# Pooled attention and routed experts: pinned pooling of the last two batches, one routing step per chunk for the second pair, another buffer for the fourth row tile

## The chip, the core and the metric

The kernel runs on one core of a Trainium2 chip. A core has five engines that each work through a list of instructions in order and wait for each other by semaphores: TensorE (PE, matrix products; PEld is its weight load), VectorE (DVE), ScalarE (ACT), GpSimd (POOL) and SyncE (SP), which here only issues DMAs. DMAs issued by GpSimd take time on that engine; most of them here are indirect: a column of indices says which rows are read or written. The metric is device time in microseconds, the median of three runs.

## What is computed

Attention comes first, over 8 batches, 8 heads, 576 positions of 64 values, with keys and values averaged over 8 neighbours:

```python
k_p = k.reshape(B, H, Sp, pool, D).mean(axis=3)        # 576 -> 72 positions
v_p = v.reshape(B, H, Sp, pool, D).mean(axis=3)
scores = scale * np.matmul(q, k_p.transpose(0, 1, 3, 2))
attn = np.exp(scores - np.max(scores, axis=-1, keepdims=True))
attn = attn / (np.sum(attn, axis=-1, keepdims=True) + 1e-09)
attn_out = np.matmul(attn, v_p)
```

Its output, as 4608 tokens of 512 values, is routed to 2 of 8 experts. The two are the largest of `x @ w_gate + log1p(exp(x @ w_noise)) * noise`, their weights a softmax of the two values:

```python
for e in range(E):
    for k in range(2):
        mask = top2[:, k] == e
        h = np.maximum(x[mask] @ w1[e], 0.0)           # 512 -> 1024
        out[mask] += top2_w[mask, k, None] * (h @ w2[e])
```

## The kernel before

A scheduling layer takes the instructions in program order with priorities and writes one list for each engine; `tc.issue_after(x)` says that what is made inside it may not stand ahead of `x`. What decides at run time is the list of each engine and the semaphores.

**Attention.** The 8 batches go in 4 pairs (`pr` 0 to 3) of 9 chunks each, so chunk `i` runs from 0 to 35; chunks 9 to 17 are the second pair, 18 to 26 the third, 27 to 35 the last. A chunk is 128 query rows of one batch, or the 64 last rows of both batches of a pair. For each, TensorE makes scores (`qk`), VectorE their maxima (`mx`), ScalarE the exponentials, TensorE transposes and multiplies with the values (`et`, `av`), and VectorE normalises into `xr` (L419), which goes to `x_dram`, and into the routing logits `lg`.

Keys and values are pooled by VectorE adds: `k_prep` and `v_prep` call `pooled` (L241, L248), three steps for `k`, four for `v`. The batch's results are needed when its pair begins. A table `bg`, filled by `plan`, says in which chunk each step is handed to the scheduler, some chunks ahead of use. The loads of `k` and `v` have two buffers each. `k7` and `v7` are the last batch's.

**Routing.** `route` makes the top two experts of a pair's 1152 tokens: a list of some 50 small VectorE steps with four `yield`s, then a count of places by two matmuls `rk` (L575, L576) that need its step L554, then the positions `pos` (L600). It is advanced by `adv` once in every chunk of the following pair, by one or two steps. When it is through, 18 indirect DMAs from GpSimd (`scatter`, L603) write the token numbers and weights of the pair into `rec_dram`. They are queued in `scq` and handed out `ADV[pr]` per chunk. `load_recs` reads these records back: for the first expert's first tiles after the second pair, for its next tiles after the third, and for all experts after the last (its `late` part: `xf`, L653, on GpSimd; `px`, L647, on TensorE).

**Experts.** Each expert has 1216 token places: four row tiles (0 to 3), three (4 to 6), and tiles 7 to 9, of which the last is half. Expert 0 takes the groups in the order 0, 4, 7; the others 0, 7, 4. For a group, `fetch` gathers token rows `xg` from `x_dram` (L702: four quarter-row gathers a tile; GpSimd), `split` transposes them and makes high and low parts, `stage1` makes `ph` (L943; three buffers), from which ScalarE and VectorE make `hh` and `hl` (L949), and `stage2` makes `py`. Then the weighted sum is put into the output rows. For experts 1 to 7 the former rows are needed: `prev` gathers them (L963) into one of three buffers `pvb`, `finish` adds on VectorE (L980) and writes back by a scatter (L984). The group of tiles 7 to 9 has its own buffer `pv4` of ten quarter-row blocks: ten gathers (L998), ten sums (L1021), ten scatters (L1024). GpSimd issues all of these in the order of its list. A group of four tiles calls `prev` for the first three at its start, and for the fourth when the first has been written back.

Of the kernel before, what the change touches and what calls it, by code (L numbers as in the profile page):

```python
# [20 lines left out]
def kernel(  # L21
# [13 lines left out]
    B, H, S, D = q.shape  # L35
# [3 lines left out]
    P = 128  # L39
# [7 lines left out]
    NP = B // 2  # L47
# [83 lines left out]
    lastx, laste, lastt = [None], [None], [None]  # L131
# [4 lines left out]
    KO, VO, PO = (5,4,2)  # L136
# [19 lines left out]
    ADV = (3,3,3,4)  # L156
# [592 lines left out]
    def plan(i, f):  # L749
        bg.setdefault(max(0, i), []).append(f)  # L750

    def nxt(store, make, b):
        def f():
            if b not in store:
                store[b] = make(b)
            next(store[b], None)
        return f

    def k1_step():
        with tc.issue_after(v0_end[0].ins):  # L760
            nxt(kg, k_prep, 1)()
# [26 lines left out]
    for b in range(1, B):  # L788
        c = 9 * (b // 2) + (0 if b % 2 == 0 else 4)
        kd = c - 2  # L790
        for x in range(KSTEPS):
            plan(kd - KO + x, nxt(kg, k_prep, b) if b > 1 else k1_step)
        for x in range(VSTEPS):
            plan(kd - VO + x, nxt(vg, v_prep, b))
        for x in range(4):
            plan(kd - PO + x, nxt(pg, pe_prep, b))
    qtr(units[0], 0)
# [21 lines left out]
    for i, (ui, u, jj) in enumerate(chunks):  # L819
        pr, ci = divmod(i, NCH)  # L820
        if ci == 0:
            lgs[pr] = rp.tile([P, NCH, H, 2 * E], F32, tag="lg", name=f"lg{pr}")
        single = u[0] == "R"
        has = ui + 1 < NU
        if single:
            order = OR
        else:
            order = OD[jj]
        eT = None
        def bgs():  # L830
            for f in bg.get(i, ()):
                f()

        def adv():
            advance(2 if pr >= NP - 2 else 1, ADV[pr])

        for o in order + ("" if "b" in order else "b") + ("" if "x" in order else "x"):
            if o == "v" and i == 0:
                drain(pg[0])
            if o == "b":  # L840
                bgs()
            elif o == "x":
                adv()
            elif o == "e":
                eT, at = et(u, jj)
            elif o == "v":
                av(u, jj, ci, eT, at, lgs[pr])
            elif o in "012":
                if has:
                    qk(units[ui + 1], int(o))  # L850
            elif ui + 2 < NU:
                qtr(units[ui + 2], "qr".index(o))
        if i >= ZS and (i - ZS) % ZD == 0 and (i - ZS) // ZD < 36 // ZW:
            if ZA:
                with tc.issue_after(lastx[0].ins):
                    zero((i - ZS) // ZD)
            else:
                zero((i - ZS) // ZD)
        if pr == NP - 1 and ci == 0:
            for ih in ((0, 0), (0, 1), (1, 0)):  # L860
                wload(0, *ih)
            early_w = chain(weights(0, 0), weights(0, 1))
        if pr == NP - 1 and 3 <= ci < 6:
            with tc.issue_after(laste[0].ins), tc.issue_after(lastx[0].ins):
                next(early_w)
                next(early_w)
            if ci == 3:
                wload(0, 1, 1)
        if pr == 3 and ci == 4:
            fetch(groups[0])  # L870
        if ci == 4 and pr >= HS:
            gens.append(route(pr, 0, 5, lgs[pr], one))
        if ci == NCH - 1 and pr < NP - 1:
            gens.append(route(pr, 5 if pr >= HS else 0, NCH, lgs[pr], one))
# [48 lines left out]
    npv = [0]  # L923
# [33 lines left out]
        HT[grp] = hs  # L957

    def prev(e, t, np_):
        pv = pvb[npv[0] % 3]  # L960
        npv[0] += 1
        if e:
            g = nc.gpsimd.indirect_dma_start(  # L963
                out=pv[:np_], out_offset=None, in_=out,
                in_offset=bass.IndirectOffsetOnAxis(ap=tokc[e, t][:np_], axis=0),
                bounds_check=NTOK - 1, oob_is_err=False)
            tc.declare_no_dep(g.ins, group=f"out{e}", reason="rows of other tokens")
            tc.add_to_no_dep_group(f"out{e}", g.ins)
        return pv

# [2 lines left out]
    def finish(e, t, np_, y, pv):  # L973
# [4 lines left out]
        for u in range(4):  # L978
# [5 lines left out]
        s = nc.gpsimd.indirect_dma_start(  # L984
            out=out, out_offset=bass.IndirectOffsetOnAxis(ap=tokc[e, t][:np_], axis=0),
            in_=res[:np_], in_offset=None, bounds_check=NTOK - 1, oob_is_err=False)
        tc.declare_no_dep(s.ins, group=f"out{e}", reason="rows of other tokens")
        tc.add_to_no_dep_group(f"out{e}", s.ins)

    def stage2(grp, mid, hook=None):  # L990
        e, t0, nt = grp
# [2 lines left out]
        if t0 == 7:  # L994
# [22 lines left out]
            for i in range(10):  # L1017
# [4 lines left out]
                else:  # L1022
# [1 line left out]
                s = nc.gpsimd.indirect_dma_start(  # L1024
                    out=out4, out_offset=bass.IndirectOffsetOnAxis(ap=oi4[e, t0 + i // 4][:, i % 4], axis=0),
                    in_=r4[:, i], in_offset=None, bounds_check=4 * NTOK - 1, oob_is_err=False)
                tc.declare_no_dep(s.ins, group=f"out{e}", reason="rows of other tokens")
                tc.add_to_no_dep_group(f"out{e}", s.ins)
            return
        pvs = [prev(e, t, P) for t in range(t0, t0 + min(nt, 3))]  # L1030
        mid()
        for t in range(t0, t0 + nt):
            cs = slice((t - t0) * P, (t - t0 + 1) * P)
# [5 lines left out]
                                                start=(i == 0), stop=(i == 3 * NFB - 1))  # L1039
                    i += 1  # L1040
            finish(e, t, P, py, pvs.pop(0))
            if t + 3 < t0 + nt:
                pvs.append(prev(e, t + 3, P))
            if hook:
                hook(t - t0)

# [182 lines left out]
```

## Time and profile before

| | |
|---|---|
| median of three runs | 1074.07 us (1072.03 to 1075.58) |
| the profiled execution | 1070.93 us, its span 1068.8 us |
| mean granted clock of TensorE | 0.983 |
| busy: TensorE, VectorE, GpSimd | 95%, 53%, 59% of the span |

The span counts from the first to the last instruction of that one execution. A granted clock of 1.00 is 2.4 GHz, 0.50 is 1.2 GHz. A time in the rows counts from the start of the span. Matmuls are pipelined, so that the ends of neighbouring rows overlap by a little. The attention ends near 201 us; the experts take the rest.

### The profile page before, as it was taken

How to read it: one execution, taken by the hardware profiler on the slowest of the kernel's cores; microseconds unless marked ns; L12 is line 12 of the kernel's file. 1: busy time of each engine (PE TensorE's matmuls, PEld its weight loads, DVE VectorE, ACT ScalarE, POOL GpSimd, SP SyncE). 2: the span in 40 equal slices, each digit the busy share in tenths (PEclk: the TensorE clock that was granted, in tenths of full speed). 3: DMA queues.
4: the chain of work that ended last, by engine and by line, in shares of the span. 5: the costliest groups of instructions: out<-in, count | busy, mean ns of one | idle time of the engine just before them, and what ended most of it. 6: DMA issues, size and time to landing. Idle time of an engine off the chain costs nothing. (4 is left out here: it accounts for less than half of the span.)

```text
span 1068.8 us, 16011 instructions
## 1 busy us (share of the span) xinstructions
PE 1020.6 (95%) x5840; PEld 920.4 (86%) x5840; DVE 565.2 (53%) x1316; ACT 340.2 (32%) x857; POOL 634.7 (59%) x662
## 2 busy tenths in 40 slices
PE   6989599899999799999999999999999999999997
PEld 5888498679898699889988998898889889988995
DVE  6888867763365146435633554355525553554241
ACT  5777577611123023212330233122312231222110
POOL 4003653746767767775677577757775777677231
PEclk8999899999999989999999999999999999999999
DMA  9999997732434243523352335233433443232200
GB/s 275 301 306 270 250 293 243 145 99 53 125 80 137 68 124 80 170 65 121 85 169 69 116 91 160 84 102 112 143 92 93 110 135 121 66 106 82 69 19 31
DMA packets 76244, 140.63 MB, mean 132 GB/s; under 512 B 24453, under 2 KB 32730, under 8 KB 76164
## 3 DMA queue, kind: packets, MB, share of 16 engines
q1 hardware_dynamic: 47844, 76.82, 26.4%
q0 software_dynamic: 28320, 62.77, 20.2%
q8 instruction: 47, 0.77, 0.3%
q14 instruction: 33, 0.27, 0.1%
HBM read 102.27 MB, written 39.17 MB: 132 GB/s over the span
## 5 line engine op out<-in xcount | busy, mean ns | idle before, releaser
L943 PE MATMUL ph<-xh,w 128*128 128x384 f32 (+2 forms) x1536 | 408.0, 347 | 8.3 <-DVE hl L949 7.7
L702 POOL DMA_INDIRECT xg<-x_dram,x x266 | 259.4, 975 | 132.2 <-issue 67.3
L943 PEld LDWEIGHTS ph<-xh,w 128*128 128x128 f32 x1536 | 277.0, 189 | 29.2 <-DVE hl L949 7.9
L948 ACT ACTIVATE hh<-ph 128x512 fp32r<-128x512 f32 (+2 forms) x192 | 97.7, 509 | 576.0 <-PE ph L943 575.3
L1038 PE MATMUL py<-w,hh 128*128 128x512 f32 x896 | 276.6, 390 | 0.0
L943 PE MATMUL ph<-xl,w 128*128 128x320 f32 (+2 forms) x768 | 266.1, 346 | 0.0
L949 DVE SCALAR_TENSOR_TENSOR hl<-ph,hh 128x512 fp32r<-128x512 f32 (+2 forms) x192 | 111.1, 579 | 215.9 <-ACT hh L948 215.8
L1038 PEld LDWEIGHTS py<-w,hh 128*128 128x128 f32 x896 | 168.0, 188 | 34.4
L1038 PE MATMUL py<-w,hl 128*128 128x512 f32 x448 | 174.6, 390 | 0.0
L943 PEld LDWEIGHTS ph<-xl,w 128*128 128x128 f32 x768 | 145.6, 190 | 10.5 <-DVE xl L917 0.2
L980 DVE SCALAR_TENSOR_TENSOR pv<-py,raw,pv 128x128 f32<-128x128 f32 x196 | 54.9, 343 | 146.5 <-PE py L1038 104.5
L1024 POOL DMA_INDIRECT out_dram<-pv,o x80 | 85.5, 1069 | 49.7 <-DVE pv L1021 25.9
L1010 PE MATMUL py<-hh,w 128*128 128x320 f32 x512 | 112.8, 309 | 0.0
L603 POOL DMA_INDIRECT rec_dram<-rec,pos x72 | 75.8, 1053 | 48.0 <-DVE pos L600 21.6
L1038 PEld LDWEIGHTS py<-w,hl 128*128 128x128 f32 x448 | 84.1, 188 | 17.4
L477 DVE TENSOR_TENSOR w<-wst,w 128x512 fp32r<-128x512 f32 x128 | 87.9, 689 | 0.8 <-ACT w L476 0.3
L1010 PEld LDWEIGHTS py<-hh,w 128*128 128x128 f32 x512 | 85.6, 188 | 0.0
L998 POOL DMA_INDIRECT pv<-out_dram,o x70 | 71.4, 1019 | 21.3 <-issue 19.8
L984 POOL DMA_INDIRECT out_dram<-pv,raw x56 | 58.1, 1038 | 41.9 <-DVE pv L980 23.0
L476 ACT CAST w<-wst 128x512 fp32r<-128x512 f32 x128 | 77.3, 616 | 6.8 <-PE ph L943 2.9
L1010 PE MATMUL py<-hl,w 128*128 128x320 f32 x256 | 79.1, 309 | 0.0
L377 ACT ACTIVATE ex<-s,mx 128x72 f32<-128x72 f32 x288 | 69.8, 347 | 12.7 <-DVE mx L375 12.3
(154 smaller groups left out, 994.4 us busy)
## 6 DMA issues: line engine op xcount, KB each, us to landing
wst<-in_moe_w_dram SPq DMA_DIRECT2D x64, 512.0 KB, 3.8
v<-in_v_dram SPq DMA_DIRECT2D x24, 448.0 KB, 13.3
out_dram<-zt SPq DMA_DIRECT2D x9, 1024.0 KB, 21.8
k<-in_k_dram SPq DMA_DIRECT2D x7, 1280.0 KB, 16.5
q<-in_q_dram SPq DMA_DIRECT2D x7, 1024.0 KB, 19.3
x_dram<-xr POOLq DMA_DIRECT2D x12, 512.0 KB, 8.6
xg<-x_dram,x POOLq DMA_INDIRECT x276, 2.6
x_dram<-xr SPq DMA_DIRECT2D x4, 512.0 KB, 6.1
```

The source lines that it names most:

```text
L377: laste[0] = nc.scalar.activation(ex[:, jj, EPOS[h] * G:(EPOS[h] + 1) * G], sv[:, i], AF.Exp, bias=mx[:, i:i + 1])
L476: nc.scalar.copy(hv, sv)
L477: nc.vector.tensor_sub(lv, sv, hv.bitcast(F32))
L603: s = nc.gpsimd.indirect_dma_start(out=rec_dram[:, :], out_offset=bass.IndirectOffsetOnAxis(ap=pos[:, i, c:c + 1], axis=0), in_=rec[:, c, ...
L702: nc.gpsimd.indirect_dma_start(out=xg[:, r * P:(r + 1) * P], out_offset=None, in_=x4, in_offset=bass.IndirectOffsetOnAxis(ap=xi[e, t][:, r ...
L943: nc.tensor.matmul(ph[:, :n], w1s(e, a, db, f), xs[b][:, db, :n], start=(i == 0), stop=(i == 3 * NDB - 1))
L948: ra = nc.scalar.activation(hh[:, :n], ph[:, :n], AF.Relu)
L949: rd = hli[grp, f] = nc.vector.scalar_tensor_tensor(hl[:, :n], ph[:, :n], 0.0, hh[:, :n].bitcast(F32), op0=OP.max, op1=OP.subtract)
L998: g = nc.gpsimd.indirect_dma_start(out=pv4[:, i], out_offset=None, in_=out4, in_offset=bass.IndirectOffsetOnAxis(ap=oi4[e, t0 + i // 4][:, ...
L1010: nc.tensor.matmul(py[:, :n], w2s(e, b, f)[:, mb * P:(mb + 1) * P], hs[f][a][:, :n], start=(i == 0), stop=(i == 3 * NFB - 1))
L1024: s = nc.gpsimd.indirect_dma_start(out=out4, out_offset=bass.IndirectOffsetOnAxis(ap=oi4[e, t0 + i // 4][:, i % 4], axis=0), in_=r4[:, i], ...
L1038: lastm[0] = nc.tensor.matmul(py, hs[f][a][:, cs], w2s(e, b, f), start=(i == 0), stop=(i == 3 * NFB - 1))
```

## The change

There are three edits. In the first, the pooling steps of the last two batches (`b >= B - 2`) are made inside `issue_after(lx[max(lx) - 2])`: they may not stand ahead of the output `xr` of the chunk two before the one that hands them out. In the second, `adv` advances the routing by two steps per chunk in the last pair alone; in the pair before it, where the second pair is routed, by one. In the third, the former rows of the fourth row tile go into the first 512 columns of `pv4`, so that its `prev` can be issued with the other three; its scatter is put into a group of its own (`outb`), so that the ten quarter-row gathers, which overwrite `pv4`, wait for it.

```diff
--- before.py
+++ after.py
@@ -756,6 +756,14 @@
             next(store[b], None)
         return f
 
+    lx = {}
+
+    def pinned(f):
+        def g():
+            with tc.issue_after(lx[max(lx) - 2]):
+                f()
+        return g
+
     def k1_step():
         with tc.issue_after(v0_end[0].ins):
             nxt(kg, k_prep, 1)()
@@ -789,9 +797,9 @@
         c = 9 * (b // 2) + (0 if b % 2 == 0 else 4)
         kd = c - 2
         for x in range(KSTEPS):
-            plan(kd - KO + x, nxt(kg, k_prep, b) if b > 1 else k1_step)
+            plan(kd - KO + x, pinned(nxt(kg, k_prep, b)) if b >= B - 2 else nxt(kg, k_prep, b) if b > 1 else k1_step)
         for x in range(VSTEPS):
-            plan(kd - VO + x, nxt(vg, v_prep, b))
+            plan(kd - VO + x, pinned(nxt(vg, v_prep, b)) if b >= B - 2 else nxt(vg, v_prep, b))
         for x in range(4):
             plan(kd - PO + x, nxt(pg, pe_prep, b))
     qtr(units[0], 0)
@@ -832,7 +840,7 @@
                 f()
 
         def adv():
-            advance(2 if pr >= NP - 2 else 1, ADV[pr])
+            advance(2 if pr == NP - 1 else 1, ADV[pr])
 
         for o in order + ("" if "b" in order else "b") + ("" if "x" in order else "x"):
             if o == "v" and i == 0:
@@ -845,6 +853,7 @@
                 eT, at = et(u, jj)
             elif o == "v":
                 av(u, jj, ci, eT, at, lgs[pr])
+                lx[i] = lastx[0].ins
             elif o in "012":
                 if has:
                     qk(units[ui + 1], int(o))
@@ -957,14 +966,18 @@
         HT[grp] = hs
 
     def prev(e, t, np_):
-        pv = pvb[npv[0] % 3]
-        npv[0] += 1
+        if t == 3:
+            pv = pv4[:, :4].rearrange("p i c -> p (i c)")
+        else:
+            pv = pvb[npv[0] % 3]
+            npv[0] += 1
         if e:
             g = nc.gpsimd.indirect_dma_start(
                 out=pv[:np_], out_offset=None, in_=out,
                 in_offset=bass.IndirectOffsetOnAxis(ap=tokc[e, t][:np_], axis=0),
                 bounds_check=NTOK - 1, oob_is_err=False)
-            tc.declare_no_dep(g.ins, group=f"out{e}", reason="rows of other tokens")
+            for gr in (f"out{e}", f"outb{e}"):
+                tc.declare_no_dep(g.ins, group=gr, reason="rows of other tokens")
             tc.add_to_no_dep_group(f"out{e}", g.ins)
         return pv
 
@@ -984,8 +997,9 @@
         s = nc.gpsimd.indirect_dma_start(
             out=out, out_offset=bass.IndirectOffsetOnAxis(ap=tokc[e, t][:np_], axis=0),
             in_=res[:np_], in_offset=None, bounds_check=NTOK - 1, oob_is_err=False)
-        tc.declare_no_dep(s.ins, group=f"out{e}", reason="rows of other tokens")
-        tc.add_to_no_dep_group(f"out{e}", s.ins)
+        for gr in (f"out{e}", f"outb{e}"):
+            tc.declare_no_dep(s.ins, group=gr, reason="rows of other tokens")
+        tc.add_to_no_dep_group(f"outb{e}" if t == 3 else f"out{e}", s.ins)
 
     def stage2(grp, mid, hook=None):
         e, t0, nt = grp
@@ -1024,10 +1038,11 @@
                 s = nc.gpsimd.indirect_dma_start(
                     out=out4, out_offset=bass.IndirectOffsetOnAxis(ap=oi4[e, t0 + i // 4][:, i % 4], axis=0),
                     in_=r4[:, i], in_offset=None, bounds_check=4 * NTOK - 1, oob_is_err=False)
-                tc.declare_no_dep(s.ins, group=f"out{e}", reason="rows of other tokens")
+                for gr in (f"out{e}", f"outb{e}"):
+                    tc.declare_no_dep(s.ins, group=gr, reason="rows of other tokens")
                 tc.add_to_no_dep_group(f"out{e}", s.ins)
             return
-        pvs = [prev(e, t, P) for t in range(t0, t0 + min(nt, 3))]
+        pvs = [prev(e, t, P) for t in range(t0, t0 + nt)]
         mid()
         for t in range(t0, t0 + nt):
             cs = slice((t - t0) * P, (t - t0 + 1) * P)
@@ -1039,8 +1054,6 @@
                                                 start=(i == 0), stop=(i == 3 * NFB - 1))
                     i += 1
             finish(e, t, P, py, pvs.pop(0))
-            if t + 3 < t0 + nt:
-                pvs.append(prev(e, t + 3, P))
             if hook:
                 hook(t - t0)
```

What this does to the lists is shown at three places. The first is VectorE in the third pair, around L554 of the routing of the second pair (`rt1`). `k7` and `v7` are the last batch's loads, `rec1` the records' weights. Before:

```order
L241 TENSOR_TENSOR k7_1394<-k7_1394 128x5x256
L542 SCALAR_TENSOR_TENSOR rt1_0_15_1611<-eidx_111,rt1_0_15_1611 128x72
L565 TENSOR_SCALAR rt1_0_20_1688<-rt1_0_19_1622 128x9
L241 TENSOR_TENSOR k7_1394<-k7_1394 128x5x128
L543 TENSOR_REDUCE rt1_0_9_1598<-rt1_0_15_1611 128x9
L567 RECIPROCAL rec1_0_1619<-rt1_0_20_1688 128x9
L545 SCALAR_TENSOR_TENSOR rt1_0_16_1615<-eidx_111,rt1_0_9_1598 128x72
L568 TENSOR_TENSOR rec1_0_1619<-rec1_0_1619,rt1_0_19_1622 128x9
L241 TENSOR_TENSOR v7_1518<-v7_1518 112x3x256
L554 TENSOR_TENSOR rt1_0_17_1617<-rt1_0_12_1605,rt1_0_16_1615 128x72
L241 TENSOR_TENSOR v7_1518<-v7_1518 112x3x256
```

The same place after:

```order
L539 TENSOR_REDUCE rt1_0_14_1673<-rt1_0_13_1671 128x9
L241 TENSOR_TENSOR v6_1275<-v6_1275 112x6x128
L541 TENSOR_TENSOR rt1_0_15_1675<-rt1_0_13_1671,rt1_0_14_1673 128x72
L557 TENSOR_TENSOR rt1_0_18_1684<-rt1_0_14_1673,rt1_0_10_1663 128x9
L542 SCALAR_TENSOR_TENSOR rt1_0_15_1675<-eidx_111,rt1_0_15_1675 128x72
L414 TENSOR_SCALAR rd2_4_2_0_1803<-a2_4_2_0_1734 128x8
L543 TENSOR_REDUCE rt1_0_9_1662<-rt1_0_15_1675 128x9
L415 RECIPROCAL rd2_4_2_0_1803<-rd2_4_2_0_1803 128x8
L545 SCALAR_TENSOR_TENSOR rt1_0_16_1679<-eidx_111,rt1_0_9_1662 128x72
L419 TENSOR_TENSOR xr2_4_2_0_1806<-a2_4_2_0_1734,rd2_4_2_0_1803 128x512
L554 TENSOR_TENSOR rt1_0_17_1681<-rt1_0_12_1669,rt1_0_16_1679 128x72
L375 TENSOR_REDUCE mx2_5_0_2_1772<-s2_5_0_2_1769 128x4
```

The adds on `k7` and `v7` no longer stand ahead of L554; one on `v6` does. Chunk 22's output (`xr2_4_2_0`, L419), which before stood behind L554, now stands ahead of it.

The second place is TensorE, at the matmuls `rk1` that take L554's result. `a2_4_1_1` are the products of chunk 21, `a2_4_2_0` those of chunk 22. Before:

```order
L408 MATMUL a2_4_1_0_1625<-vbd0_168,eT2_4_1_0_1624 128x81 x2
L394 MATMUL a2_4_1_1_1722<-ident_69,ex2_4_1_0_1477 112x128 x2
L394 MATMUL a2_4_2_0_1770<-ident_69,ex2_4_2_0_1635 112x128 x2
L575 LDWEIGHTS ones_109
L575 MATMUL rk1_0_1694<-rt1_0_17_1617,ones_109 128x72
L576 LDWEIGHTS before_104
L576 MATMUL rk1_0_1694<-rt1_0_17_1617,before_104 128x72
L394 MATMUL ep2_4_1_1_0_1723<-ident_69,ex2_4_1_0_1477 112x128 x4
L344 MATMUL qp2_5_0_0_1734<-ident_69,q5_1272 128x128 x4
L408 MATMUL a2_4_1_1_1722<-vbd0_168,eT2_4_1_1_1721 128x162 x2
```

And after:

```order
L408 MATMUL a2_4_2_0_1734<-vbd0_168,eT2_4_2_0_1733 64x162 x4
L408 MATMUL a2_4_2_0_1734<-vbd0_168,eT2_4_2_0_1733 64x81 x2
L408 MATMUL a2_4_2_0_1734<-vbd1_170,eT2_4_2_0_1733 64x162 x4
L408 MATMUL a2_4_2_0_1734<-vbd1_170,eT2_4_2_0_1733 64x81 x2
L370 MATMUL s2_5_0_2_1769<-kbd1_166,qT2_5_0_1698 128x144 x2
L575 LDWEIGHTS ones_109
L575 MATMUL rk1_0_1818<-rt1_0_17_1681,ones_109 128x72
L576 LDWEIGHTS before_104
L576 MATMUL rk1_0_1818<-rt1_0_17_1681,before_104 128x72
L394 MATMUL ep2_5_0_0_0_1847<-ident_69,ex2_5_0_0_1744 112x128 x3
```

`rk1` has moved from ahead of chunk 21's products to behind those of chunk 22.

The third place is GpSimd in the first group of expert 2, as it stands in experts 2 to 6 alike: gathers of former rows into `pv0` to `pv2`, scatters to the output from them, the ten gathers into `pv4`, and row gathers `xg3` for expert 3. The first of the gathers of the group stands one row ahead. Before:

```order
L963 DMA pv0_2647<-out_0_dram,raw0_8_0_3095 128x512
L963 DMA pv1_2648<-out_0_dram,raw0_8_0_3095 128x512
L998 DMA pv4_2650<-out_0_dram,o0_8_0_3170 128x128 x10
L702 DMA xg3_0_5242<-x_dram_67,x0_8_0_3184 128x128 x4
L702 DMA xg3_1_5247<-x_dram_67,x0_8_0_3184 128x128 x4
L984 DMA out_0_dram<-pv2_2649,raw0_8_0_3095 4608x512
L963 DMA pv2_2649<-out_0_dram,raw0_8_0_3095 128x512
L702 DMA xg3_2_5252<-x_dram_67,x0_8_0_3184 128x128 x4
L984 DMA out_0_dram<-pv0_2647,raw0_8_0_3095 4608x512
L963 DMA pv0_2647<-out_0_dram,raw0_8_0_3095 128x512
L984 DMA out_0_dram<-pv1_2648,raw0_8_0_3095 4608x512
L963 DMA pv1_2648<-out_0_dram,raw0_8_0_3095 128x512
```

And after, behind the gathers into `pv0`, `pv1` and `pv2`:

```order
L975 DMA pv4_2650<-out_0_dram,raw0_8_0_3095 128x512
L702 DMA xg3_0_5242<-x_dram_67,x0_8_0_3184 128x128 x4
L702 DMA xg3_1_5247<-x_dram_67,x0_8_0_3184 128x128 x4
L997 DMA out_0_dram<-pv0_2647,raw0_8_0_3095 4608x512
L702 DMA xg3_2_5252<-x_dram_67,x0_8_0_3184 128x128 x4
L975 DMA pv0_2647<-out_0_dram,raw0_8_0_3095 128x512
L997 DMA out_0_dram<-pv1_2648,raw0_8_0_3095 4608x512
L975 DMA pv1_2648<-out_0_dram,raw0_8_0_3095 128x512
L997 DMA out_0_dram<-pv2_2649,raw0_8_0_3095 4608x512
L975 DMA pv2_2649<-out_0_dram,raw0_8_0_3095 128x512
L997 DMA out_0_dram<-pv4_2650,raw0_8_0_3095 4608x512
L1012 DMA pv4_2650<-out_0_dram,o0_8_0_3170 128x128 x10
```

Before, the fourth gather is the one into `pv2` that follows the scatter from `pv2`. Now it goes into `pv4` and follows the first three; the ten gathers into `pv4` have moved from ahead of the row gathers to behind the fourth scatter, which now reads `pv4`.

## Rows read from the trace of the kernel before

**Rows 1.** The page, part 1: busy us (share of the span) xinstructions.

```profile
PE 1020.6 (95%) x5840; PEld 920.4 (86%) x5840; DVE 565.2 (53%) x1316; ACT 340.2 (32%) x857; POOL 634.7 (59%) x662
```

**Rows 2.** Waits of TensorE: engine, line, waited for; us in total, times, longest.

```profile
PE rk L575 <- DVE rt L554: 9.8, 2, 9.2
PE ph L943 <- DVE hl L949: 7.7, 1, 7.7
```

**Rows 3.** Timeline, TensorE, three places: start us, us, what, count [idle before <-releaser].

```profile
131.72 0.22 PE L575 MATMUL rk<-rt,ones 128*128 128x72 bf16 x1 [9.21 <-DVE rt L554]
...
259.56 1.12 PE L647 MATMUL px<-xf,sel 128*128 128x80 f32 x8
...
374.63 0.64 PE L943 MATMUL ph<-xh,w 128*128 128x320 f32 x1 [7.67 <-DVE hl L949]
```

**Rows 4.** Windows: stretch, length, busy time (x instructions) by engine, granted clock, DMA share, GB/s.

```profile
68.50:114.30 45.80, 40.96 (x346) 37.82 (x347) 38.54 (x112) 33.99 (x118) 15.01 (x15) 1.00 1.05 275
120.90:167.20 46.30, 35.07 (x265) 33.18 (x265) 31.92 (x93) 25.08 (x87) 25.42 (x26) 0.85 1.05 298
131.70:137.20 5.50, 4.80 (x21) 4.36 (x21) 4.21 (x20) 1.99 (x4) 0.00 (x0) 0.50 1.03 340
374.60:380.10 5.50, 5.47 (x21) 5.47 (x22) 2.56 (x5) 0.95 (x2) 4.28 (x5) 0.51 0.29 86
400.00:500.00 100.00, 100.00 (x522) 89.69 (x521) 51.27 (x101) 25.80 (x50) 69.14 (x69) 1.00 0.38 113
```

**Rows 5.** Timeline, VectorE, 106 to 168 us.

```profile
106.71 1.48 DVE L241 TENSOR_TENSOR k<-k 128x1280 f32<-128x1280 f32 x1
...
120.94 0.68 DVE L419 TENSOR_TENSOR xr<-a,rd 128x512 f32<-128x512 f32 x1
...
130.57 0.96 DVE L241 TENSOR_TENSOR v<-v 112x768 f32<-112x768 f32 x1 [2.04 <-DMA v<-in_v_dram]
131.44 0.23 DVE L554 TENSOR_TENSOR rt<-rt,rt 128x72 bf16<-128x72 f32 x1
...
150.27 0.69 DVE L419 TENSOR_TENSOR xr<-a,rd 128x512 f32<-128x512 f32 x1
...
167.19 0.69 DVE L419 TENSOR_TENSOR xr<-a,rd 128x512 f32<-128x512 f32 x1
```

**Rows 6.** Timeline, GpSimd (POOL), 106 to 259 us.

```profile
106.47 2.57 POOL L603 DMA_INDIRECT rec_dram<-rec,pos  x1 [0.30 <-issue]
...
137.75 1.03 POOL L603 DMA_INDIRECT rec_dram<-rec,pos  x1 [8.54 <-DVE pos L600]
...
171.53 0.59 POOL L633 DMA_DIRECT2D raw<-rec_dram  x1 [7.12 <-DMA rec_dram<-rec,pos]
...
181.98 0.60 POOL L429 DMA_DIRECT2D x_dram<-xr  x1
...
188.34 1.02 POOL L603 DMA_INDIRECT rec_dram<-rec,pos  x1 [5.76 <-DVE pos L600]
...
258.88 0.62 POOL L653 CAST xf<-raw 128x80 f32<-128x80 int32 x1
```

**Rows 7.** Timeline, VectorE, experts 1 and 2, 373 to 478 us.

```profile
373.06 1.12 DVE L980 SCALAR_TENSOR_TENSOR pv<-py,raw,pv 128x128 f32<-128x128 f32 x4 [15.64 <-DMA pv<-out_dram,raw]
...
400.78 2.72 DVE L1021 SCALAR_TENSOR_TENSOR pv<-yt,w,pv 128x128 f32<-128x128 f32 x10
...
477.75 1.13 DVE L980 SCALAR_TENSOR_TENSOR pv<-py,raw,pv 128x128 f32<-128x128 f32 x4 [5.31 <-DMA pv<-out_dram,raw]
```

**Rows 8.** Timeline, GpSimd, experts 1 and 2, 342 to 450 us.

```profile
342.25 1.22 POOL L963 DMA_INDIRECT pv<-out_dram,raw  x1 [2.17 <-issue]
...
369.51 1.02 POOL L963 DMA_INDIRECT pv<-out_dram,raw  x1 [0.31 <-DMA xg<-x_dram,x]
...
445.41 1.04 POOL L963 DMA_INDIRECT pv<-out_dram,raw  x1 [2.57 <-issue]
...
449.38 1.00 POOL L998 DMA_INDIRECT pv<-out_dram,o  x1 [0.30 <-issue]
```

## The prediction

> **What bounds the kernel now.** The page comes first: TensorE is busy 1020.6 of 1068.8 us [rows 1]. So only the 48 us in which it is idle, and the stretches at the lower clock, can be won; no matmul of the sum is changed. The waits of TensorE come next: two of them are 9.2 and 7.7 us in one piece [rows 2], and the diff touches both places. The timeline dates them. The first ends at 131.72, where the ranking matmul `rk` waits for the last step of VectorE's routing list, L554; the second ends at 374.63, where a matmul of expert 1's second group waits for `hl` [rows 3]. Windows just behind each show a granted clock of 0.50 and 0.51, the 1.2 GHz level, for 5.5 us [rows 4]; each stall so costs a further 5.5 x 0.5 = 2.7 us of lost pace. From 400 to 500 us TensorE is busy 100.00 of 100 [rows 4]: in the later experts nothing is to be won, only lost.
>
> Why the first stall: on VectorE the row before L554 is a pooling add of `v`, which waited 2.04 us for its load and began at 130.57; L554 could only follow at 131.44 [rows 5]. TensorE, with `rk` at its head, stood still meanwhile. Why the second: VectorE stood 15.64 us before the weighted sum at 373.06, for the gather of the fourth row tile's former rows [rows 7], which GpSimd issued only at 369.51 [rows 8], behind ten quarter-row gathers and seven row gathers. VectorE works in order, so `hl` waited behind that sum.
>
> **Part 1, pooling pinned and routing at one step per chunk.** The order shows that the adds on `k7` and `v7` and the last on `v6` leave the place ahead of L554, and that `rk` stands behind chunk 22's products instead of ahead of chunk 21's. By the time the new order reaches the first add on `v7`, behind chunk 23, that piece, which was being waited for until 130.57 [rows 5], has landed. So the stall and its 2.7 us of low clock go. The adds themselves stay; they ran under the stall and now lie among the chunks. The nearest stretch with such adds and a route in it is 68.50 to 114.30, nine chunks in 45.80 us, 5.09 a chunk, at 41.0 us busy TensorE and 38.5 us busy VectorE [rows 4]. Chunk 20's output begins at 120.94, chunk 27's at 167.19 [rows 5]: seven chunks in 46.25 us. At 5.09 they take 35.6, and chunk 27 comes at 156.6, **10.6 us earlier**. Bounds: nothing faster than TensorE's own 35.07 us busy there less the 2.7 of low clock, 32.4, so 13.9 earlier; and if the adds cost their full sum again behind what waits, some 5.
>
> What is late next: the records. GpSimd writes each pair's 18 token records, loads them back, and only then turns to the next pair. In the trace the second pair's records begin at 137.75, their load goes out at 171.53, and the queue is free when the `x` write at 181.98 ends, 182.58, 44.8 us after the start; the third pair's begin at 188.34, having waited 5.76 us for VectorE's positions [rows 6]. From there the queue runs through to `xf` at 258.88, and the matmul `px` begins at 259.56, with `xf` just finished at 259.50 [rows 6, 3]: no slack at all. The changed order has the second pair's positions right behind chunk 23's output. Chunk 23 comes at 120.94 + 3 x 5.09 = 136.2 instead of 150.27 [rows 5], the positions some 2.3 us later, the first record at about 139: one step per chunk makes them no earlier than before. With the same 44.8 us, and 1.6 us for a pooling add that catches a record write (the one at 106.47 took 2.57 beside the `k` add of 106.71, against 1.03 at 137.75 [rows 6, 5]), the queue is free at 185.4. The positions of the third pair, 10.6 us earlier at 177.7, then wait for it. Records, loads and `xf` come 188.34 - 185.4 = 2.9 us earlier, while TensorE reaches `px` 10.6 earlier: it waits about 7.7 us there and, as after the 7.67 us wait, loses 2.7 at the low clock. **Net of part 1: -2.9 + 2.7 = -0.2 us.** Bounds: if the queue is free by 177.7, the whole 10.6 comes through; if the positions come at 144 and the queue is free at 191, `px` begins 2.7 later, and with the low clock it is +5.4.
>
> [...]
>
> **Part 2, the fourth row tile in the quarter-row buffer.** The four gathers of former rows stand together; the fourth waits for no scatter of the first tile. For expert 1 it leaves GpSimd three places behind the first gather at 342.25, so at some 1.32 us each ((449.38 - 445.41) / 3 [rows 8]) at about 346.2, 23 us sooner than it did. The 7.67 us and the 2.7 us of low clock go: **-10.4 us**. Bounds: 0 if another wait takes the place, -10.4 at best. In expert 0 the fourth tile has no gather and gains only a buffer. In experts 2 to 7 VectorE waited up to 5.31 us for the same gather [rows 7] with TensorE never idle: nothing.
>
> What it adds: the ten quarter-row gathers share the buffer, so they now stand behind the fourth tile's scatter and wait for it to land. Behind them on GpSimd stand twelve row gathers for the next expert and ten scatters. In expert 1 the fourth sum is ready at about 373.06 - 10.4 = 362.7, but its scatter has 22 places ahead of it (4 gathers, 12 row gathers, 3 scatters, 3 gathers for the third group): 342.25 + 22 x 1.32 = 371.3. A landing as ahead of the first gather of expert 2 (2.57 us [rows 8]), then 10 x 1.32, end near 387; with a landing again, near 390. They are needed at 400.78 [rows 7] less the 10.4 won, 390.4, and one by one from there, 0.27 us apart. So this just fits. In expert 2 the same steps from 445.41, with some 8 us more for row buffers that VectorE frees only behind its first group, give 500; needed are they one expert (445.41 - 342.25 = 103 us) after 400.78, near 504. Should they be a few us late, VectorE waits but TensorE still has three `ph` buffers to fill. Cost taken: 0.
>
> **The sum.** The profiled execution took 1070.93 us for a span of 1068.8: 1070.93 - 0.2 - 10.4 = 1060.3. The median of the runs, 1074.07, stands 3.1 us higher, so the forecast is **1063.5**.
>
> **Rivals.**
> 1. *Records keep up.* The queue is free by 177.7, because the loads that make records land late (the wait of 7.12 us [rows 6]) thin out. Then -10.6 - 10.4 = -21.0: 1053. Against it: the DMA share is 1.05 over the whole of 120.9 to 167.2 [rows 4], and work pulled earlier does not empty a full queue.
> 2. *Records later.* One step per chunk puts the positions at 144 instead of 139: +5.4 - 10.4 = -5.0: 1069. For it: the VectorE order between chunks 22 and 24 is crowded with nine `base` adds, `k7` and `vs6`.
> 3. *The late gather is replaced by another.* Part 2 returns nothing, as `hl` then waits for the next thing, say the row gathers; part 1 -0.2: 1074. Against it: in experts 2 to 7 the same sequence runs with TensorE 100.00 of 100 busy.
> 4. *Slower: the ten gathers come too late in every expert.* Place: VectorE's L1021 in the second group of experts 1 to 7. GpSimd now stands at row gathers that wait for VectorE's transposes before it reaches the fourth scatter. With landing near 500 against 504, and some 6 us of `ph` buffers, it decides from about 10 us of further delay; beyond that each us costs seven times. The gain of 10.4 is used up by 1.5 us per expert; at 3 us and 2.7 of low clock it is 7 x 5.7 - 10.4 = +29.5: 1103.
>
> **How the numbers follow.** Forecast as summed 0.50, records keep up 0.20, records later 0.12, gather replaced 0.09, too late in every expert 0.09. What a measurement of this kernel can tell from no change is 0.3%, 3.2 us, so faster is under 1070.9. Of the first case nearly all is faster, of the second all, of the third most, of the fourth little: 0.49 + 0.20 + 0.08 + 0.01 = 0.78. Same: 0.01 + 0.04 + 0.08 = 0.13; slower 0.09. The range goes from the second case's 1053 to the top of the third, 1071; the likeliest case alone is 1058 to 1068.
>
> **What would show it.** Right: the waits of TensorE no longer name `rk` with 9 us, nor `hl` with 7.7; a wait of several us stands at `px` for `xf`, with 5 us of clock near 0.5 behind; the GpSimd queue runs without an idle piece from the second pair's records to `xf`. Part 1 is wrong if chunk 27 is less than 5 us earlier, or if `px` waits for nothing and comes 10 earlier. Part 2 is wrong if TensorE stands in expert 1's second group, or L1021 waits for its gathers long enough to reach TensorE. The forecast falls if the time is above 1071 or under 1053.

## The result, and the profile after

The changed kernel took **1060.96 us** (median of 14 runs, 1055.44 to 1068.21) where the kernel before took 1073.6 (14 runs, 1070.42 to 1077.83): a ratio of **0.9884, 95% interval [0.986, 0.9909]**. Measured once more for the last experiment, it took 1054.97 us (6 runs), 0.9819 [0.9789, 0.9849] of the kernel before, which took 1074.14 beside it. A ratio leaves out runs more than 1.5% above the fastest of their kernel, which only one chip had (four experiments below). The first profiled execution took 1062.75 us for a span of 1060.7.

The page, part 1, answers to [rows 1]: the work is the same, and the idle time of TensorE has gone from 48 to 37 us.

```profile
PE 1023.5 (96%) x5840; PEld 922.5 (87%) x5840; DVE 564.6 (53%) x1316; ACT 340.6 (32%) x857; POOL 638.5 (60%) x662
```

The waits of TensorE (in total, times, longest), to be held against [rows 2]: `hl` is gone, `rk` is down to 0.8 us, and three new names stand at the top.

```profile
PE px L647 <- POOL xf L653: 4.3, 1, 4.3
PE xp L915 <- DMA xg<-x_dram,x: 3.8, 4, 1.7
PE ep L394 <- DVE rt L592: 3.7, 1, 3.7
...
PE rk L575 <- DVE rt L554: 0.8, 1, 0.8
```

The timeline of TensorE, for [rows 3]. `px` begins at 259.41, against 259.56 before: the attention's gain has been waited away in front of it.

```profile
132.18 0.21 PE L575 MATMUL rk<-rt,ones 128*128 128x72 bf16 x1 [0.79 <-DVE rt L554]
...
140.91 0.65 PE L394 MATMUL ep<-ident,ex 128*112 128x128 f32 x4 [3.73 <-DVE rt L592]
...
259.41 2.00 PE L647 MATMUL px<-xf,sel 128*128 128x80 f32 x8 [4.32 <-POOL xf L653]
```

Windows, columns as in [rows 4]: behind the wait at `px` 5.5 us at half clock; where the wait for `hl` stood, and in all later experts, TensorE is never idle.

```profile
259.40:264.90 5.50, 5.49 (x23) 5.49 (x24) 1.04 (x3) 0.00 (x0) 4.20 (x5) 0.53 0.42 121
...
350.00:400.00 50.00, 50.00 (x301) 47.62 (x300) 21.86 (x48) 9.18 (x19) 35.78 (x36) 1.00 0.34 99
400.00:500.00 100.00, 100.00 (x527) 89.67 (x526) 49.47 (x99) 24.32 (x47) 72.48 (x73) 1.00 0.39 115
```

VectorE, for [rows 5, 7]: the outputs of chunks 20, 23 and 27, and in expert 1 the fourth sum, now waiting for TensorE alone, and the ten sums, waiting for nothing.

```profile
120.95 0.68 DVE L419 TENSOR_TENSOR xr<-a,rd 128x512 f32<-128x512 f32 x1
...
139.95 0.69 DVE L419 TENSOR_TENSOR xr<-a,rd 128x512 f32<-128x512 f32 x1 [3.15 <-DMA x_dram<-xr]
...
160.16 0.69 DVE L419 TENSOR_TENSOR xr<-a,rd 128x512 f32<-128x512 f32 x1
...
363.97 1.13 DVE L993 SCALAR_TENSOR_TENSOR pv<-py,raw,pv 128x128 f32<-128x128 f32 x4 [4.31 <-PE py L1053]
...
392.68 2.72 DVE L1035 SCALAR_TENSOR_TENSOR pv<-yt,w,pv 128x128 f32<-128x128 f32 x10
```

GpSimd, for [rows 6, 8]: the records' chain, then in expert 1 the fourth gather and the first and last of the ten quarter-row gathers.

```profile
143.09 2.41 POOL L603 DMA_INDIRECT rec_dram<-rec,pos  x1 [9.94 <-DVE pos L600]
...
181.33 0.58 POOL L633 DMA_DIRECT2D raw<-rec_dram  x1 [9.64 <-DMA rec_dram<-rec,pos]
...
192.30 1.01 POOL L603 DMA_INDIRECT rec_dram<-rec,pos  x1 [0.31 <-issue]
...
259.11 0.25 POOL L653 CAST xf<-raw 128x80 f32<-128x80 int32 x1
...
348.63 1.00 POOL L975 DMA_INDIRECT pv<-out_dram,raw  x1 [0.31 <-issue]
...
377.92 1.01 POOL L1012 DMA_INDIRECT pv<-out_dram,o  x1 [3.85 <-DMA out_dram<-pv,raw]
...
390.36 0.99 POOL L1012 DMA_INDIRECT pv<-out_dram,o  x1 [0.30 <-issue]
```

So the profile splits at `px`. Up to `px`: 259.41 - 259.56 = -0.15 us. From `px` to the end: 1060.7 - 259.41 = 801.3 against 1068.8 - 259.56 = 809.2, -7.9 us, which is the 10.4 of part 2 less 2.5 for half clock behind the wait. This split is the yardstick for the experiments, since every edit but part 2 lies ahead of `px`.

### The profile page after: what moved, and what is told of

Read it like the earlier page. It is cut to its first block, busy times and chain, and to the rows that moved or that the text cites. A ratio compares the mean times of both kernels' runs of the same rounds, so it can differ in the third digit from the quotient of the medians.

```text
span 1060.7 us, 16002 instructions
## 1 busy us (share of the span) xinstructions
PE 1023.5 (96%) x5840; PEld 922.5 (87%) x5840; DVE 564.6 (53%) x1316; ACT 340.6 (32%) x857; POOL 638.5 (60%) x662
## 5 line engine op out<-in xcount | busy, mean ns | idle before, releaser
L952 PEld LDWEIGHTS ph<-xl,w 128*128 128x128 f32 x768 | 145.2, 189 | 10.6
L1012 POOL DMA_INDIRECT pv<-out_dram,o x70 | 75.0, 1071 | 37.6 <-issue 18.6
L997 POOL DMA_INDIRECT out_dram<-pv,raw x56 | 59.8, 1067 | 52.1 <-DVE pv L993 31.9
```

The costliest lines, as they stand in the source:

```text
L952: nc.tensor.matmul(ph[:, :n], w1s(e, a, db, f), xs[b][:, db, :n], start=(i == 0), stop=(i == 3 * NDB - 1))
L1012: g = nc.gpsimd.indirect_dma_start(out=pv4[:, i], out_offset=None, in_=out4, in_offset=bass.IndirectOffsetOnAxis(ap=oi4[e, t0 + i // 4][:, ...
```

## The experiments

The theory to test (A): part 2 is worth its 10.4 us; part 1 shortens the attention, but TensorE then stands at `px` for the records' chain on GpSimd. The rivals: the parts share the gain, or the pinning or the routing rate alone makes it.

| kernel | median us (runs) | ratio to before, 95% | `px` begins | from `px` to the end |
|---|---|---|---|---|
| before | 1073.6 (14) | - | 259.56 | 809.2 |
| changed | 1060.96 (14) | 0.9884 [0.986, 0.9909] | 259.41 | 801.3 |
| changed, again | 1054.97 (6) | 0.9819 [0.9789, 0.9849] | 252.21 | 798.9 |
| part 2 alone | 1064.37 (6) | 0.9907 [0.9878, 0.9936] | 264.98 | 798.7 |
| part 1 alone | 1065.3 (10) | 0.9929 [0.9905, 0.9953] | 252.50 | 808.3 |
| changed, two routing steps | 1059.79 (6) | 0.9872 [0.9843, 0.9901] | 259.32 | 798.8 |
| changed, not pinned | 1053.99 (6) | 0.984 [0.9801, 0.988] | 249.57 | 798.9 |
| changed, `px` later | 1050.47 (6) | 0.9775 [0.9741, 0.9808] | 258.43 | 792.5 |
| not pinned, `px` later | 1050.24 (6) | 0.9775 [0.9744, 0.9806] | 254.97 | 792.5 |
| part 2 alone, `px` later | 1062.05 (6) | 0.989 [0.986, 0.992] | 264.40 | 792.5 |

The last two columns are from one profiled execution each. Each ratio is to runs of the kernel before on the same chip, and the chips differ: the four versions from part 2 alone to not pinned ran on chip 0, the changed and the unpinned kernel with `px` later on chip 11, part 2 alone with `px` later and the changed kernel's second measurement on chip 15; the chip of its first is not on record. The changed kernel's two ratios lie 0.65% apart, so differences between rows of different chips are no surer than that. With `px` later some 6.3 us of matmuls stand ahead of it that stood behind (798.8 - 792.5).

### Part 2 alone

The kernel before, with the diff's edits in `prev`, `finish` and `stage2` and none of the others.

> The kernel before with the fourth row tile's former rows in the quarter-row buffer and nothing else. Theory A (the record chain on GpSimd takes back all that the attention stages gain, so the whole gain is this part's): -7.7 us of wait for hl and -2.7 us of half clock behind it, 1073.6 - 10.4 = about 1063, ratio 0.990, and px waits 0 as before. Rival B (the two parts share the gain: an earlier stage lets the mixture of experts begin sooner): 1066 to 1069, ratio 0.993 to 0.996. Rival C (the ten quarter-row gathers behind the fourth scatter are late once the rest is unchanged): 1070 or more.

1064.37 us, ratio 0.9907. TensorE waits for `rk`, now in two pieces worth naming, and for nothing at `px` or `hl`. The first line is from its waits; the second is the later of the two pieces in the timeline, and the third the window behind it, with the granted clock as the last figure but two:

```profile
PE rk L575 <- DVE rt L554: 10.3, 2, 7.1
...
224.00 0.24 PE L575 MATMUL rk<-rt,ones 128*128 128x72 bf16 x1 [3.18 <-DVE rt L554]
...
223.90:229.40 5.50, 5.40 (x15) 4.24 (x16) 3.46 (x20) 0.60 (x1) 3.00 (x3) 0.50 0.41 117
```

From `px` to the end it took 798.7 us, 10.5 less than before: part 2 is worth what was summed for it. `px` itself came 5.4 us later than in the profile of before, and not through the attention, whose last output begins at 201.08 us (200.72 before). The `rk` of the last pair, behind it, waited 3.18 us instead of 0.62, and lost some 2.7 us more at the low clock, 5.3 in all. VectorE, on its way to L554, had stood 3.14 us there for a step of ScalarE (L512), against 1.23 before. With `px` later (the last experiments) the same `rk` waited 1.83 us and the clock stayed at 1.00, so this differs between executions.

### Part 1 alone

The kernel before with the first two edits of the diff and not the third (lines shortened; the definition of `pinned` is left out):

```diff
+                av(...); lx[i] = lastx[0].ins
+            plan(kd - KO + x, pinned(nxt(kg, k_prep, b)) if b >= B - 2 else ...)
+            plan(kd - VO + x, pinned(nxt(vg, v_prep, b)) if b >= B - 2 else ...)
+            advance(2 if pr == NP - 1 else 1, ADV[pr])
```

> The kernel before with pinned pooling and one routing step per chunk and nothing else. Theory A: the rk wait of 9.2 us goes, TensorE waits about 4 us at px and about 4 us at xp instead, so 1073 to 1074, ratio 0.999 to 1.001, and the 7.7 us wait for hl in expert 1 is still there. Rival B: 1067 to 1071, ratio 0.994 to 0.998, with px reached earlier than 258 us.

1065.3 us, ratio 0.9929: theory A's 1073 to 1074 fell, and it is a little below the rival's 1067 to 1071. The waits, first of all and then the one at `px`:

```profile
PE ph L952 <- DVE hl L958: 7.7, 1, 7.7
PE xp L915 <- DMA xg<-x_dram,x: 4.5, 2, 3.4
...
PE px L647 <- POOL xf L653: 2.2, 1, 2.2
```

TensorE does wait at `px`, but `px` begins at 252.50, 7 us sooner than before. The wait at `px` is real and takes a part of the gain, not the whole.

### The two halves of part 1

Two routing steps per chunk again, pooling still pinned:

```diff
-            advance(2 if pr == NP - 1 else 1, ADV[pr])
+            advance(2 if pr >= NP - 2 else 1, ADV[pr])
```

> The changed kernel with two routing steps per chunk for the third pair again (pooling stays pinned). Theory A (the pinned pooling alone clears VectorE ahead of rk, the slower routing is not needed and costs the records time): positions of the second pair before 140 us instead of 142.6, third pair's records earlier by 2 to 4 us, px earlier by as much, 1057 to 1060. Rival B (with two steps the counts come before their data as in the kernel before): a wait of 5 to 9 us at rk returns and the time is 1061 to 1064, since px is set by the records.

1059.79 us, as theory A had it, but not by its way. The first waits of TensorE:

```profile
PE ep L394 <- ACT ex L377: 3.9, 2, 3.8
PE rk L575 <- DVE rt L554: 3.1, 1, 3.1
```

The timeline of GpSimd (the first record of the third pair, the first record of the last pair, and `xf`), and `px` on TensorE.

```profile
182.09 1.02 POOL L603 DMA_INDIRECT rec_dram<-rec,pos  x1 [0.71 <-DVE pos L600]
...
226.22 1.00 POOL L603 DMA_INDIRECT rec_dram<-rec,pos  x1 [6.97 <-DVE nt L1140]
...
257.04 0.25 POOL L653 CAST xf<-raw 128x80 f32<-128x80 int32 x1
...
259.32 1.01 PE L647 MATMUL px<-xf,sel 128*128 128x80 f32 x8
```

The second pair's positions came at 130.24 and the third pair's records at 182.09, both earlier. Yet `px` came at 259.32, and not for want of its records: `xf` had ended at 257.29, and TensorE did not wait. TensorE was late itself. The stall at `rk`, at 127 us, put chunk 27 at 162.69. In the last pair VectorE waited 4.78 us before chunk 32's output (at 190.13) for the write of an older `xr` buffer to land, and TensorE stood 3.76 us at `ep` behind it; the last output of the attention began at 199.87, against 188.68 in the changed kernel's second profile. The last pair's positions (225.77), which follow the end of the attention, held GpSimd for 6.97 us, so `xf` too gained little. So `px` is set by the record queue where it waits, and by TensorE's own way through the attention where it does not. In this one profile two steps help the first and spoil the second; whether the wait at chunk 32 belongs to them is open, since the changed kernel's first profile has one of 3.15 us at chunk 23 and its second has none.

The pooling not pinned, one step kept (the line for `v` is changed likewise; the first line is shortened):

```diff
-            plan(kd - KO + x, pinned(nxt(kg, k_prep, b)) if b >= B - 2 else ...)
+            plan(kd - KO + x, nxt(kg, k_prep, b) if b > 1 else k1_step)
```

> The changed kernel with the pooling not pinned (one routing step per chunk and the fourth row tile stay). Theory A (the slower routing alone keeps TensorE from rk's wait, while the pooling adds ahead of it on VectorE make the positions later): rk waits under 3 us, positions of the second pair at 143 to 148 us, px 1 to 5 us later than in the changed kernel, 1061 to 1067. Rival B (pinning does nothing): within 1 us of the changed kernel, positions at the same 142.6 us.

1053.99 us: neither theory's numbers. `rk` has no wait worth a row; the second pair's positions come at 138.22, not at 143 or later.

This reads as 7 us won by leaving the pinning out, against the first measurement of the changed kernel; against its second (1054.97) it is 1 us, and the intervals overlap both times. Beside two steps, the pinning gives 1059.79 where part 2 alone gave 1064.37, on the same chip; there too the intervals overlap.

### Four runs on another chip

The next four were to repeat the changed kernel and the unpinned one, and to place `px` later in both (`LF = 2` to `LF = 5`).

> The changed kernel once more, for a second profile of it beside the next three. Theory A (where px falls is set by how soon the records land while the DMA engines are full, and it differs from run to run): the same 1061 within 3 us, px somewhere between 251 and 262 us, and from px to the end 799 to 802 us again. Rival B (the 3.15 us wait for an xr buffer at chunk 23 belongs to the change): it is there again, with chunk 23 at 139 to 141 us.

> The changed kernel without the pinning once more. Theory A (the pinned adds put the second pair's positions 2 to 4 us later, and the records' chain hands that on to px): 1054 within 3 us, 5 to 9 us below the changed kernel of the same call, positions of the second pair at 138 us, px at 248 to 253 us. Rival B (the first measurement was a lucky one): within 3 us of the changed kernel.

> The changed kernel with the spreading matmuls px and pw placed behind the sixth block of expert 0's second first-stage group instead of the third (some 6 us later on TensorE). Theory A (the records' chain costs the end only because TensorE stands at px): the wait of 4.3 us at px and the half clock behind it go, 1061 - 4.3 - 2.5 = 1054. Rival B (expert 1's gathers, which need px, then come late and TensorE stands at expert 1's first block instead): 1059 to 1063.

> Both edits: no pinning, and px behind the sixth block. Theory A (each takes its own piece: the attention ends 3 to 5 us earlier and px never waits): 1054 - 1.7 - 1 = about 1051, and a smaller scatter than the kernel without pinning had (1050 to 1064). Rival B (both remove the same wait): 1053 to 1056.

They took 1311.24, 1317.0, 1313.73 and 1314.65 us, and the kernel before, on the same chip, 1307.3 (1281.91 to 1325.02): that chip ran every version some 22% slower. None of the four was faster than the kernel before there: the ratios are 1.0128, 1.0197, 1.0192 and 1.0135, each with an interval of 0.010 to 0.013 either way. In the changed kernel's profile TensorE waited for `issue`, which names no other engine, in over a hundred places of the experts:

```profile
PE ph L952 <- issue: 44.3, 51, 2.1
PE py L1024 <- issue: 42.9, 63, 1.7
```

The runs of one version spread over 1.1 to 3.3%, so nothing of 1% can be read, and that the change gains anything on such a chip is not shown. Why that chip took longer is open. Three of the four were measured again on other chips.

### `px` later

```diff
-    LF = 2
+    LF = 5
```

In the changed kernel:

> The changed kernel with the spreading matmuls px and pw placed behind the sixth block of expert 0's second first-stage group instead of the third (some 6 us later on TensorE). Theory A (the records' chain costs the end only because TensorE stands at px): no wait at px, no half clock at 259 to 264 us, 1061 - 4.3 - 2.5 = 1054. Rival B (expert 1's gathers, which need px, then come late and TensorE stands at expert 1's first block instead): 1059 to 1063.

In the changed kernel without the pinning:

> No pinning, and px behind the sixth block. Theory A (the pinning costs by itself, in the attention: chunk 27 at 154 us instead of 157 to 160, the second pair's positions at 138 us instead of 140 to 143): 3 to 5 us below the pinned kernel with the same px, 1049 to 1052, no wait at px. Rival B (all that the unpinned kernel gained was a shorter wait at px): within 2 us of the pinned kernel with the same px.

In the kernel before with part 2 alone:

> Only the fourth row tile's edit, with px behind the sixth block; pooling and routing as in the kernel before. Theory A (px waits only because the attention now ends sooner than the records): nothing to remove here, 1063 to 1066 as with that part alone, and pinned pooling with one routing step is worth 12 to 16 us once px is out of its way (1064.4 against 1050.5). Rival B (a later px gains by itself): 1054 to 1059, and the pooling and routing edit is worth less than 8 us.

They took 1050.47, 1050.24 and 1062.05 us. In the first there is no wait at `px` any more; its largest is 3.5 us at `qp`, in the attention. The timeline of both engines: `xf` on GpSimd, and `px` on TensorE, which begins 4.4 us after `xf` is there.

```profile
253.78 0.25 POOL L653 CAST xf<-raw 128x80 f32<-128x80 int32 x1
...
258.43 1.01 PE L647 MATMUL px<-xf,sel 128*128 128x80 f32 x8
```

Three things follow. Expert 1's gathers can bear a later `px`: 792.5 us from there to the end is the same in all three. With part 2 alone the later `px` gives nothing that can be told (0.9907 to 0.989): there was no wait to remove, so the wait is made by part 1, and by its routing step: the kernel that is not pinned waits 1.7 us at `px`, the pinned one with two steps does not wait. And part 1, with `px` out of its way, is worth 0.989 - 0.9775 = 1.15% of 1073, 12.3 us, with intervals that do not touch. The rival's 1054 to 1059 falls with 1062.05; its bound of 8 us is not far outside the error, as the two ratios are from different chips, and in the profiles `px` begins only 6.0 us earlier (258.43 against 264.40). For the pinning the medians are as the rival had them: with `px` later the pinned and the unpinned kernel differ by 0.2 us. The intervals leave room for some 5 us either way, so theory A's 3 to 5 us is not ruled out. The size of the gain over the changed kernel as given is less sure: 10.5 us against its first measurement, 4.5 against its second.

### The changed kernel again

> The changed kernel once more. Theory A (a wait for the records at px in most executions, whose length goes with how soon the records land): 1058 to 1063, from px to the end 799 to 802 us, TensorE waiting 2 to 6 us at px or just through. Rival B (the first profile was an odd one, px mostly finds its records): 1056 or less.

1054.97 us. The wait at `px` is there, 2.4 us, but the time is as rival B had it, below 1056. The first profile was no odd execution among its own: it took 1062.75 us beside a median of 1060.96. The two measurements differ as a whole. GpSimd, the same places as in the result, with the third pair's load and the first `x` index behind it:

```profile
140.47 2.41 POOL L603 DMA_INDIRECT rec_dram<-rec,pos  x1 [6.75 <-DMA x_dram<-xr]
...
174.59 0.57 POOL L633 DMA_DIRECT2D raw<-rec_dram  x1 [7.61 <-DMA rec_dram<-rec,pos]
...
185.15 1.00 POOL L603 DMA_INDIRECT rec_dram<-rec,pos  x1 [0.30 <-issue]
...
207.27 1.03 POOL L603 DMA_INDIRECT rec_dram<-rec,pos  x1 [0.30 <-issue]
...
215.28 0.59 POOL L633 DMA_DIRECT2D raw<-rec_dram  x1 [6.98 <-DMA rec_dram<-rec,pos]
217.22 0.24 POOL L672 TENSOR_SCALAR x<-raw 128x3 int32<-128x3 int32 x1 [1.35 <-DMA raw<-rec_dram]
...
251.91 0.25 POOL L653 CAST xf<-raw 128x80 f32<-128x80 int32 x1
```

VectorE in the same execution, the outputs of chunks 20 and 27:

```profile
121.53 0.68 DVE L419 TENSOR_TENSOR xr<-a,rd 128x512 f32<-128x512 f32 x1
...
156.88 0.68 DVE L419 TENSOR_TENSOR xr<-a,rd 128x512 f32<-128x512 f32 x1
```

TensorE at `px`:

```profile
252.21 1.12 PE L647 MATMUL px<-xf,sel 128*128 128x80 f32 x8 [2.44 <-POOL xf L653]
```

## Why the prediction came out, point by point

**The total.** 1063.5 was forecast; 1060.96 and 1054.97 were measured, both inside 1053 to 1071, and faster. That the first came so near is in part luck. Up to `px` its profile is 0.15 us sooner where the sum had 2.9: the third pair's records came 4.0 us later instead of 2.9 sooner, the chain behind them was 3.7 us shorter than the sum held it, and `xf` was done 0.4 us faster.

**Part 2, -10.4: right in place and size.** From `px` to the end the span fell from 809.2 to 798.7 to 798.9 in every version with this part, with `px` in its old place and without a long wait there. The fourth gather was expected at 346.2; it left at 348.63, as expected three places behind the first, which itself left 2.2 us later (344.48). The ten gathers were to just fit: the last left at 390.36, and the sums that use them ran from 392.68 without a wait. Rivals 3 and 4 did not occur; TensorE is busy 100.00 of 100 from 400 to 500 us, and with part 1 alone the wait of 7.7 us for `hl` is still there.

**Part 1, the attention: right in size.** Chunks 20 to 27 were to take 35.6 us instead of 46.25. In the second profile of the changed kernel they take 156.88 - 121.53 = 35.35, and 35.3 with part 1 alone. In the first it was 39.2: there VectorE waited 3.15 us before chunk 23's output for the write of an older `xr` buffer to land, and TensorE behind it 3.73 us at `ep`. No other of the profiles on the faster chips has that wait at chunk 23. The prediction gave the gain to both halves together. By the profiles each half shortens the stretch by itself: one step without pinning takes 33.9 us (154.33 - 120.40), pinning with two steps 40.3; part 2 alone, with neither, 46.9, and 43.6 with `px` later. Beside the one step the pinning adds nothing there.

**Part 1, the records: right in kind.** The third pair's records were forecast at 185.4; they came at 185.15, 187.37 with part 1 alone, and 192.30 in the first profile. The first record write, beside the moved `k` and `v` adds (on VectorE from 140.29 and 141.03), took 2.41 us, and another 1.48, against 1.0 for most: 1.9 us more, where 1.6 had been put in. By the Trainium skill, SBUF — State Buffer, "Who interferes with whom", a VectorE instruction with two SBUF inputs contends with a GpSimd instruction that reads SBUF. The trace agrees in the first write; no run moved the adds alone.

**The term that was mis-sized: part 1's net, -0.2.** Alone it measured 1065.3 against 1073.6, -7.6 us by the ratio (interval -5.1 to -10.2), inside the bounds of -10.6 and +5.4 but far from the value taken. The step that failed is "From there the queue runs through to `xf`": it held the 70.5 us from the third pair's first record (188.34) to `xf` (258.88) fixed. With part 1 they are 64.8 to 66.8 (251.91 - 185.15). Rows of the kernel before for the same places as above:

```profile
212.00 1.08 POOL L603 DMA_INDIRECT rec_dram<-rec,pos  x1 [0.30 <-issue]
218.80 0.58 POOL L633 DMA_DIRECT2D raw<-rec_dram  x1 [5.72 <-DMA rec_dram<-rec,pos]
223.74 0.24 POOL L672 TENSOR_SCALAR x<-raw 128x3 int32<-128x3 int32 x1 [4.36 <-DMA raw<-rec_dram]
```

In the second profile after, the load of the records lands 3.0 us sooner (4.36 to 1.35 us of wait), and the 18 records before it take 22.1 us instead of 23.7; from the last of them to the load it is 1.2 us longer (8.0 after, 6.8 before). So up to `px` this profile is 7.35 us sooner where the sum had 2.9: 3.2 from the start of the records, 3.8 from the chain, 0.4 from `xf` itself; and the 2.7 us of low clock did not come. In the 13 us around this load the DMA engines were busy 0.61 of the time before (212 to 225) and 0.39 after (207 to 220). With the attention done sooner, the 512 KB loads of expert weights that SyncE issues behind its outputs (`wst`) no longer stand beside the load; five of them go out from 202.84 to 217.70 before (first row), and from 190.79 to 207.81 in the changed kernel's second profile (second row):

```profile
202.84 14.86 SPq L455 DMA_DIRECT2D wst<-in_moe_w_dram  x5
...
190.79 17.02 SPq L455 DMA_DIRECT2D wst<-in_moe_w_dram  x5
```

The window of before (the DMA share is the last figure but one):

```profile
212.00:225.00 13.00, 12.38 (x57) 9.94 (x56) 11.79 (x50) 4.21 (x10) 2.19 (x4) 1.00 0.61 162
```

And of the changed kernel's second profile:

```profile
207.00:220.00 13.00, 12.57 (x57) 10.09 (x57) 11.43 (x58) 2.61 (x5) 3.37 (x5) 1.00 0.39 82
```

This is the argument that the prediction held against its first rival ("work pulled earlier does not empty a full queue"), and it was looked at in the wrong stretch: the queue was full at 120 to 167, but the load that matters lies at 218. Across the profiles the wait for this load goes with the traffic during it: 1.35 to 1.5 us at a DMA share of 0.03 or 0.04 with one step, 3.6 to 4.4 us at 0.56 to 0.73 in the kernel before, with part 2 alone and with two steps; but part 2 alone with `px` later, without part 1, had 1.73 us at 0.43. That the thinner traffic is the cause is read from these rows and not shown; no run took away the transfers alone.

**The half clock behind the wait at `px`: in one execution of two.** 2.7 us had been added for it. After 4.32 us of wait the clock stood at 0.53 for 5.5 us. After 2.44 us, in the second profile, it stayed at 1.00:

```profile
252.20:257.70 5.50, 5.49 (x37) 5.49 (x38) 1.83 (x5) 1.00 (x2) 4.21 (x5) 1.00 0.42 127
```

The length of a wait alone does not settle it: 3.18 us at `rk` in part 2 alone were followed by 5.5 us at 0.50, 3.73 us at `ep` in the first profile of the changed kernel by 0.69 over 5.5 us, and 2.31 us at `xp` in the second by 0.70.

**The rivals.** The second measurement, 1054.97, lies 2 us from "Records keep up" (1053) and 8.5 from the forecast. Its reason, that the loads thin out, is what the rows show at the third pair's load; its condition, a queue free by 177.7, is not met (185.15). "Records later" had the positions at 144; 140.01 and 142.63 were seen, and the first profile came near to it without its +5.4.

## What to carry to other kernels

When a stall goes, follow the chain that is late next with its own waits, not as a block of fixed length: a wait for a transfer in it can shrink or grow with the traffic of the stage that has been moved. A matmul that waits for a side chain and is needed only later can be put some blocks further back: here one number (`LF` from 2 to 5) brought 1050.5 us, with 1050.2 unpinned the fastest measured, and without it part 1 gave up 3 to 10 of its 12 us (0.9819 and 0.9884 against 0.9907, 9.4 and 2.5 us left). Of two edits that came together, test each alone: beside the slower routing the pinning changed nothing that the runs can tell.

## What had not been expected

- The same changed kernel measured 0.9884 [0.986, 0.9909] and 0.9819 [0.9789, 0.9849] of a kernel before that agreed within 0.6 us between the two measurements. The traces differ where the DMA engines are full: the second pair's load leaves at 181.33 in one and 174.59 in the other, and the DMA busy share from 170 to 200 us (last figure but one of a window) is 0.91 and 0.72. What makes the difference is open. The first profile:

```profile
170.00:200.00 30.00, 24.36 (x166) 20.06 (x165) 19.14 (x61) 17.87 (x55) 12.61 (x14) 0.88 0.91 256
```

The second profile:

```profile
170.00:200.00 30.00, 24.44 (x148) 20.27 (x149) 20.97 (x56) 20.38 (x60) 16.34 (x18) 0.89 0.72 201
```

- Two gains that were each measured alone, -10.0 and -7.6 us by their ratios, came together to -12.5 in one measurement and -19.4 in the other. Where a chain of transfers decides, 1% from one measurement is not the last word.
